# A fused attention + MoE kernel: second batch's softmax weights transposed by DMA, and the third expert unit's gathers ordered first

## The chip, the cores and the metric

One core of a Trainium2 chip runs the whole program. The metric is the device time of one execution in microseconds; several executions are timed and their median counts.

## The reference

Three layers follow each other on 1536 tokens (2 batches of 768) of width 512.

1. Attention with 8 heads of 64, scores `q k^T / 8` plus a bias that falls linearly with distance, kept only where the key is one of 8 global tokens or lies 0 to 95 places back; softmax; product with `v`.
2. A dense feed-forward layer: RMS norm, `silu(xn w_gate) * (xn w_val)`, times `w_out` (512 to 1536 and back).
3. A mixture of 8 experts (512 to 1024 and back, ReLU): a noisy router picks two experts per token, the token's two outputs are added with softmax weights of the two logits.

`top2 = argpartition(-noisy_logits, 2)[:, :2]` means that a small error upstream can send a token to another expert, which is why most matrix products run as three products of split halves (high x high, high x low, low x high).

## The kernel before, in words

**Attention.** Tokens come in 12 tiles `ti` of 128; tiles 0 to 5 are the first batch (`ti < F32T`), 6 to 11 the second. The eight heads of a tile are done in four pairs `pr`; a *unit* `u = 4*ti + pr` is one tile and one pair, 48 in all. A unit goes through three functions. `scores` (L409) multiplies on PE into a PSUM bank, adds the bias and finds the row minimum on DVE (L429, tile `s`), and takes the exponential on ACT (L432, tile `p`). `turn` (L437) transposes `p` on PE in blocks of 128x128 (L445): four blocks for a pair, or two where the tile is the first of its batch (one block of keys in place of two). In the second batch it then makes two half-precision tiles out of PSUM, a high part on ACT (L456) and the rest on DVE (L457). `values` (L465) multiplies these with `v` (L494, twenty products of 64 columns). When a tile's four pairs are done it is normalised (L502, then `rms`, L568) and `norm` (L586) transposes it for the next layer (tiles `xTh`, `xTl`, L595 and L596).

**Order.** `slot(n, part)` (L509) writes the order down: slot n holds `turn(n-1)`, `scores(n)` and `values(n-2)`, and at n % 4 == 2 the `norm` of the tile before. Slots 0 to 11 are written out by `early` (L536); the rest are dealt out by `side` (L1161) between the matmuls of the dense layer, eight for each of its first visits. `VISITS` (L132) lists the dense layer's visits: the first six take two token tiles each through the hidden chunks 0 to 3 (functions `up` L686, `hidden` L697, `down` L710). The framework then orders each engine's queue by a timeline of its own, so a slot can run well after the place where it is written; on the chip each queue is strictly in order. The sixth visit can't start before the last tile's `norm`.

**Loads.** SP's queue issues all plain loads and the transposing DMAs that exist already (L975 for gathered tokens `hg`, L1132 for expert outputs `ob`). The output is cleared by one 3 MB write from a zero tile (`clear_out`, L268), issued in the third visit.

**Experts.** `route` (L787) ranks the tokens of a group; for each assignment it scatters token number and weight into the table `metad` (L911, POOL). Nine `Unit`s of gathered tokens follow: units 0 and 1 are the same expert in two parts, units 2 to 8 one expert each. A unit's steps are `fetch` (L936: its part of the table, tile `me`, by SP), `slots` (L943: indices `ic` on POOL, L952), `gather` (L958: one indirect DMA from POOL per 128 tokens, from `x2d` for units up to 2, from the halved copy `x2p` for later ones), `turn` (L977: four PE transposes per 128 tokens, L990, then `gh` on ACT and `gl` on DVE, L993 and L994), and `run` (L1003) with eight steps f of `up` (L1022) and `down` (L1039, L1062). `halve` (L741) writes `x2p`: a copy on POOL into `hw` (two buffers) and a store by SP. `late` (L1233) routes the last group, halves the last four token tiles, and orders the first eight weight loads of unit 2 (`moe2_weights`, L919); then the loop at L1244 runs the units, with `side(f)` (L1248) ordering the next unit's fetch, slots, gathers, turns and weights. During unit 1 it does this for unit 2:

```
if i == 1:
    if f == 0:
        nxt.slots()
    if 1 <= f <= len(nxt.tiles):
        nxt.gather(f - 1)
```

Of the kernel before, what the change touches and what calls it, by code (L numbers as in the profile page):

```python
# [107 lines left out]
def fused(ctx: ExitStack, tc: tile.TileContext, q, k, v, n_global, n_local, w_gate, w_val, w_out,  # L108
# [55 lines left out]
    def build_bias():  # L164
        rel = sb.tile([P, 2 * P], F32, name="rel", tag="n2", bufs=N2)
        msk = sb.tile([P, 2 * P], F32, name="msk", tag="s", bufs=4)
        tmp = at.tile([P, 2 * P], F32, name="tmp", tag="p", bufs=4)
# [5 lines left out]
        rel0 = at.tile([P, P], F32, name="rel0", tag="p", bufs=4)  # L173
        msk0 = at.tile([P, P], F32, name="msk0", tag="p", bufs=4)
# [44 lines left out]
    blank = sb.tile([P, P], BF16, name="blank")  # L219
    nc.vector.memset(blank, 0.0)  # L220
# [47 lines left out]
    def clear_out():  # L268
        zero = at.tile([P, P], F32, name="zero", tag="p", bufs=4)
        nc.gpsimd.memset(zero, 0.0)  # L270
        nc.sync.dma_start(out.rearrange("(p t) (c d) -> p (t c) d", p=P, d=P),
                            zero.rearrange("p (o d) -> p o d", o=1).broadcast_to([P, NT // P * DC, P]))
# [136 lines left out]
    def scores(u, wide):  # L409
# [8 lines left out]
        pp = []  # L418
# [7 lines left out]
        for t in range(2):  # L426
# [4 lines left out]
            p = at.tile([P, 2 * P], F32, name=f"p{ti}_{h}", tag="p", bufs=4)  # L431
            state["e"] = nc.scalar.activation(p[:, :W], s[:, :W], AF.Exp, scale=-1.0, bias=mx[:, h:h + 1],  # L432
                                              accum_out=sm[:, h:h + 1]).ins
            pp.append(p)
        state["p", u] = pp

    def turn(u, wide):  # L437
# [5 lines left out]
        for t in range(2):  # L443
            for j in range(nblk):
                seq(nc.tensor.transpose(p4[:, t, j, :], pp[t][:, j * P:(j + 1) * P], ident))  # L445
        if ti < F32T:
            pf = at.tile([P, 2, 2, P], F32, name=f"pf{ti}_{pr}", tag="pt", bufs=2)
            if pr % 2 == 0:
                nc.scalar.activation(pf[:, :, :nblk], p4[:, :, :nblk], AF.Copy, scale=PSC)
            else:  # L450
                nc.vector.tensor_scalar(pf[:, :, :nblk], p4[:, :, :nblk], PSC, None, op0=ALU.mult)
            state["pt", u] = (pf[:, 0], pf[:, 1])
            return
        pair16 = at.tile([P, 2, 2, 2, P], F16, name=f"ph{ti}_{pr}", tag="pt", bufs=2)
        ph, pl = pair16[:, 0], pair16[:, 1]
        nc.scalar.activation(ph[:, :, :nblk], p4[:, :, :nblk], AF.Copy, scale=PSC)  # L456
        nc.vector.scalar_tensor_tensor(pl[:, :, :nblk], p4[:, :, :nblk], PSC, ph[:, :, :nblk],  # L457
                                       op0=ALU.mult, op1=ALU.subtract)
        state["pt", u] = (ph, pl)
# [49 lines left out]
    def slot(n, part):  # L509
# [16 lines left out]
        else:  # L526
# [4 lines left out]
            if ("pt", n - 2) in state:  # L531
# [835 lines left out]
```

## Time and profile before

| | us |
|---|---|
| median of 3 timed runs | 776.04 (775.14 to 782.92) |
| the profiled execution, device time | 777.18 |
| its span, first to last instruction | 775.5 |

The rows below come from that one execution. PE is the matmul engine, PEld its weight loads, DVE, ACT and POOL the vector, scalar and general engines, SP the engine that issues most DMAs. "busy" is the time in which at least one instruction of the engine is in flight; a matmul's duration overlaps with the next one's, so the time that one takes from PE is read from start to start. "idle before <-X" is the time the engine stood before an instruction and what released it. L numbers are lines of the kernel.

### The profile page before, as it was taken

The page shows a single profiled execution, that of the slowest core. Times are in us where ns is not written, and L with a number is a line of the kernel's source. Part 1 is how long each engine was busy: PE and PEld are TensorE (multiplying, and loading weights), DVE is VectorE, ACT ScalarE, POOL GpSimd, SP SyncE. Part 2 cuts the span into 40 slices and gives each one's busy share as a digit, 9 for nine tenths or more (in the row PEclk, how much of TensorE's full clock was granted, in tenths as well). Part 3 has the DMA queues.
Part 4 walks back from the last instruction along what each step waited for, and adds up shares of the span by engine and source line. Part 5 has one row for each costly group of instructions (what it writes and reads, how often), then busy time and mean ns, then how long its engine had stood idle before and what let it go on. Part 6 is the DMA issues. An engine that isn't in the chain of part 4 may idle for free. (4 is left out here: it accounts for less than half of the span.)

```text
span 775.5 us, 13632 instructions
## 1 busy us (share of the span) xinstructions
PE 747.3 (96%) x4851; PEld 675.6 (87%) x4851; DVE 480.6 (62%) x1104; ACT 407.1 (53%) x854; POOL 325.5 (42%) x357
## 2 busy tenths in 40 slices
PE   9899999999999999999999999799999999999993
PEld 5788989999798888889999988678999999999993
DVE  7988776766477889433535568544555656556642
ACT  6777566665444344113332455435575857676640
POOL 3367741332376557111542145352244545453511
PEclk9999999999999999999999999999999999999997
DMA  7554332250233330002243626896686989999211
GB/s 194 140 177 110 104 107 52 55 177 2 82 109 109 108 109 28 0 19 91 56 56 57 216 29 148 277 303 188 164 203 148 294 176 292 250 300 189 78 40 37
DMA packets 159864, 102.22 MB, mean 132 GB/s; under 512 B 90897, under 2 KB 142097, under 8 KB 159792
## 3 DMA queue, kind: packets, MB, share of 16 engines
q1 hardware_dynamic: 150944, 78.84, 40.2%
q0 software_dynamic: 7120, 19.32, 8.2%
q10 hardware_dynamic: 1728, 3.15, 1.5%
q8 instruction: 40, 0.66, 0.4%
q14 instruction: 32, 0.26, 0.1%
HBM read 75.23 MB, written 16.49 MB: 118 GB/s over the span
## 5 line engine op out<-in xcount | busy, mean ns | idle before, releaser
L1022 PE MATMUL pz<-gh,sa 128*128 128x256 f32 (+7 forms) x576 | 154.5, 337 | 1.5 <-ACT gh L993 0.8
L1022 PEld LDWEIGHTS pz<-gh,sa 128*128 128x128 f32 x576 | 104.1, 189 | 6.6 <-POOL sa L677 1.0
L1022 PE MATMUL pz<-gl,sa 128*128 128x256 f32 (+7 forms) x288 | 96.4, 336 | 0.8 <-DVE gl L994 0.8
L720 PE MATMUL acc<-wo,dh 128*128 128x512 f32 x288 | 89.0, 400 | 1.0 <-ACT dh L706 1.0
L1062 PE MATMUL ac<-zh,sb 128*128 128x480 f32 (+4 forms) x320 | 84.8, 357 | 0.0
L693 PE MATMUL pz<-xTh,wg 128*128 128x256 f32 x352 | 75.4, 289 | 2.3 <-ACT wg L644 1.3
L1029 ACT ACTIVATE zh<-pz 128x256 fp32r<-128x256 f32 (+7 forms) x72 | 35.1, 487 | 78.6 <-PE pz L1022 78.5
L1030 DVE SCALAR_TENSOR_TENSOR zl<-pz,zh 128x256 fp32r<-128x256 f32 (+7 forms) x72 | 39.7, 551 | 57.4 <-ACT zh L1029 57.1
L693 PE MATMUL pz<-xTh,wv 128*128 128x256 f32 x352 | 75.0, 288 | 0.0
L693 PEld LDWEIGHTS pz<-xTh,wg 128*128 128x128 f32 x352 | 59.0, 192 | 4.4 <-ACT wg L644 1.5
L1095 POOL DMA_INDIRECT out_dram<-y,me x30 | 32.5, 1083 | 72.0 <-DVE y L1091 57.8
L1062 PEld LDWEIGHTS ac<-zh,sb 128*128 128x128 f32 x320 | 59.5, 188 | 3.4 <-ACT sb L673 0.2
L677 DVE TENSOR_TENSOR sb<-wab,sb 128x512 fp32r<-128x512 f32 x67 | 47.6, 711 | 22.9 <-ACT sb L673 21.1
L707 POOL TENSOR_TENSOR dl<-u,dh 128x256 fp32r<-128x256 f32 (+1 forms) x38 | 38.6, 1015 | 53.8 <-ACT dh L706 30.1
L673 ACT ACTIVATE sa<-wab 128x512 fp32r<-128x512 f32 x72 | 44.9, 625 | 28.5 <-PE ac L1062 14.1
L720 PEld LDWEIGHTS acc<-wo,dh 128*128 128x128 f32 x288 | 51.3, 189 | 9.8 <-ACT dh L706 1.6
L693 PEld LDWEIGHTS pz<-xTh,wv 128*128 128x128 f32 x352 | 58.6, 191 | 0.4
L1022 PEld LDWEIGHTS pz<-gl,sa 128*128 128x128 f32 x288 | 54.4, 189 | 3.5 <-DVE gl L994 1.2
L432 ACT ACTIVATE p<-s,mx 128x256 f32<-128x256 f32 (+1 forms) x96 | 46.2, 483 | 21.2 <-DVE mx L429 21.1
L720 PE MATMUL acc<-wo,dl 128*128 128x512 f32 x144 | 53.0, 399 | 0.2 <-POOL dl L707 0.2
L677 DVE TENSOR_TENSOR sa<-wab,sa 128x512 fp32r<-128x512 f32 x54 | 40.1, 745 | 20.8 <-ACT sa L673 20.2
L1062 PE MATMUL ac<-zl,sb 128*128 128x480 f32 (+4 forms) x160 | 52.4, 358 | 0.0
(254 smaller groups left out, 1873.0 us busy)
## 6 DMA issues: line engine op xcount, KB each, us to landing
wab<-in_moe_w_dram SPq DMA_DIRECT2D x128, 256.0 KB, 5.4
rg<-in_moe_w_gate_dram SPq DMA_DIRECT2D x12, 512.0 KB, 4.6
rv<-in_moe_w_val_dram SPq DMA_DIRECT2D x12, 512.0 KB, 3.7
ro<-in_moe_w_out_dram SPq DMA_DIRECT2D x12, 512.0 KB, 3.5
vn<-in_v_dram SPq DMA_DIRECT2D x12, 256.0 KB, 4.6
out_dram<-zero SPq DMA_DIRECT2D x1, 3072.0 KB
x2d<-x ACTq DMA_DIRECT2D x12, 256.0 KB, 7.6
x2p<-hw SPq DMA_DIRECT2D x12, 256.0 KB, 4.5
```

The costliest lines, as they stand in the source:

```text
L432: state["e"] = nc.scalar.activation(p[:, :W], s[:, :W], AF.Exp, scale=-1.0, bias=mx[:, h:h + 1], accum_out=sm[:, h:h + 1]).ins
L673: cp = nc.scalar.activation(wp[:, 0], src, AF.Copy)
L677: (nc.gpsimd if pool else nc.vector).tensor_sub(wp[:, 1], src, wp[:, 0].bitcast(F32))
L693: mm = nc.tensor.matmul(pz, a[:, cs], x[:, tt:tt + nt, c, :], start=(n == 0), stop=(n == 3 * DC - 1))
L707: (nc.gpsimd if ci < len(CHUNKS) - 1 else nc.vector).tensor_sub(dl, u, dh.bitcast(F32))
L720: nc.tensor.matmul(acc[t], a[:, tt], w, start=(f == CHUNKS[ci][0] and n == 0), stop=(end and n == 2))
L1022: mm = nc.tensor.matmul(pz[:, :cap], a[:, cs], x[:, c, :cap], start=(k == 0), stop=(k == 3 * DC - 1))
L1029: self.act = nc.scalar.activation(dh[:, :cap], pz[:, :cap], AF.Relu).ins
L1030: nc.vector.scalar_tensor_tensor(dl[:, :cap], pz[:, :cap], 0.0, dh[:, :cap].bitcast(F32), op0=ALU.max, op1=ALU.subtract)
L1062: nc.tensor.matmul(acc[c][:, :cap], w[:, c * P:(c + 1) * P], a[:, :cap], start=(f == 0 and k == 0), stop=(f == FB2 - 1 and k == 2))
L1095: st = nc.gpsimd.indirect_dma_start(out=out, out_offset=bass.IndirectOffsetOnAxis(ap=self.me[:m, s, 0:1], axis=0), in_=y[:m], in_offset=No ...
```

## The change

Attention, second batch: after the exponential (now written over `s`), ACT makes the high half-precision part of each head from SBUF and DVE the rest, into one tile `pp` of [128, 2 parts, 2 heads, 256 columns] with two buffers; one transposing DMA on SP's queue turns this tile (eight blocks, or four for the first tile of the batch) into `both`, which `values` reads. `turn` is left for the first batch alone. `values` of the second batch moves one slot later (n-3 in place of n-2), its `norm` too, and there is one slot more. The first batch's two `p` tiles of a pair become one tile.

Third unit: in `late` its `fetch` is ordered ahead of its eight weight loads, and these are put behind the fetch in SP's queue; its `slots` and all four gathers are ordered at f = 0 of unit 1; the last four `halve` copies are put behind the last of these gathers on POOL, unit 3's `slots` behind the last copy, and unit 3's first two weight loads behind the last store of a halved tile.

Elsewhere: the 3 MB clearing write moves to the ninth visit, from a zero tile that is set once at the start and also serves as `blank`.

```diff
@@ -415,7 +413,11 @@
         mx, sm = state["mx", ti], state["sm", ti]
         nb = nbias if ti % NB else nbias0
         psc = bank("s", wide, f"ps{ti}_{pr}")
-        pp = []
+        first = ti < F32T
+        if first:
+            pp = at.tile([P, 2, 2 * P], F32, name=f"p{ti}_{pr}", tag="p", bufs=2)
+        else:
+            pp = at.tile([P, 2, 2, W], F16, name=f"h{ti}_{pr}", tag="p", bufs=2)
         for t in range(2):
             h = pair(ti, pr)[t]
             sl = slice((h % 2) * D, (h % 2 + 1) * D) if ti < HALF else slice(0, P)
@@ -428,11 +430,18 @@
             s = sb.tile([P, 2 * P], F32, name=f"s{ti}_{h}", tag="s", bufs=4)
             state["s"] = nc.vector.tensor_tensor_reduce(s[:, :W], nb[:, h, :], psc[:, t * W:(t + 1) * W], 1.0, BIG * 10,
                                                         op0=ALU.add, op1=ALU.min, accum_out=mx[:, h:h + 1]).ins
-            p = at.tile([P, 2 * P], F32, name=f"p{ti}_{h}", tag="p", bufs=4)
-            state["e"] = nc.scalar.activation(p[:, :W], s[:, :W], AF.Exp, scale=-1.0, bias=mx[:, h:h + 1],
+            p = pp[:, t, :W] if first else s[:, :W]
+            state["e"] = nc.scalar.activation(p, s[:, :W], AF.Exp, scale=-1.0, bias=mx[:, h:h + 1],
                                               accum_out=sm[:, h:h + 1]).ins
-            pp.append(p)
-        state["p", u] = pp
+            if not first:
+                nc.scalar.activation(pp[:, 0, t], p, AF.Copy, scale=PSC)
+                nc.vector.scalar_tensor_tensor(pp[:, 1, t], p, PSC, pp[:, 0, t], op0=ALU.mult, op1=ALU.subtract)
+        if first:
+            state["p", u] = pp
+            return
+        both = at.tile([P, 2, 2, nblk, P], F16, name=f"ph{ti}_{pr}", tag="pt", bufs=2)
+        nc.sync.dma_start_transpose(both.rearrange("p x t j q -> p (x t j) q"), pp.rearrange("p x t c -> p (x t c)"))
+        state["pt", u] = both[:, 0], both[:, 1]
 
     def turn(u, wide):
         ti, pr = divmod(u, NP)
@@ -442,21 +451,13 @@
         p4 = ptt.rearrange("p (t j q) -> p t j q", t=2, j=2)
         for t in range(2):
             for j in range(nblk):
-                seq(nc.tensor.transpose(p4[:, t, j, :], pp[t][:, j * P:(j + 1) * P], ident))
-        if ti < F32T:
-            pf = at.tile([P, 2, 2, P], F32, name=f"pf{ti}_{pr}", tag="pt", bufs=2)
-            if pr % 2 == 0:
-                nc.scalar.activation(pf[:, :, :nblk], p4[:, :, :nblk], AF.Copy, scale=PSC)
-            else:
-                nc.vector.tensor_scalar(pf[:, :, :nblk], p4[:, :, :nblk], PSC, None, op0=ALU.mult)
-            state["pt", u] = (pf[:, 0], pf[:, 1])
-            return
-        pair16 = at.tile([P, 2, 2, 2, P], F16, name=f"ph{ti}_{pr}", tag="pt", bufs=2)
-        ph, pl = pair16[:, 0], pair16[:, 1]
-        nc.scalar.activation(ph[:, :, :nblk], p4[:, :, :nblk], AF.Copy, scale=PSC)
-        nc.vector.scalar_tensor_tensor(pl[:, :, :nblk], p4[:, :, :nblk], PSC, ph[:, :, :nblk],
-                                       op0=ALU.mult, op1=ALU.subtract)
-        state["pt", u] = (ph, pl)
+                seq(nc.tensor.transpose(p4[:, t, j, :], pp[:, t, j * P:(j + 1) * P], ident))
+        pf = at.tile([P, 2, 2, P], F32, name=f"pf{ti}_{pr}", tag="pt", bufs=2)
+        if pr % 2 == 0:
+            nc.scalar.activation(pf[:, :, :nblk], p4[:, :, :nblk], AF.Copy, scale=PSC)
+        else:
+            nc.vector.tensor_scalar(pf[:, :, :nblk], p4[:, :, :nblk], PSC, None, op0=ALU.mult)
+        state["pt", u] = (pf[:, 0], pf[:, 1])
 
     def grows(ti):
         for a, b in zip(state["own", ti - 1], state.pop(("own", ti - 2))):
@@ -528,10 +529,13 @@
                 scores(n, wide)
             if n % NP == 1 and n // NP + 1 < NT // P:
                 prep(n // NP + 1, wide)
-            if ("pt", n - 2) in state:
+            if n - 2 < F32T * NP and ("pt", n - 2) in state:
                 values(n - 2, wide)
-        if part and n % NP == 2 and n >= NP:
-            norm(n // NP - 1, state.pop(("x", n // NP - 1)), wide)
+            if n - 3 >= F32T * NP and ("pt", n - 3) in state:
+                values(n - 3, wide)
+        ti = n // NP - 1
+        if part and n >= NP and n % NP == (2 if ti < F32T or not windowed else 3):
+            norm(ti, state.pop(("x", ti)), wide)
 
     def early(n):
 
@@ -680,6 +684,7 @@
     x2t = {}
     tail = []
     halves2 = {}
+    halved = []
     marks = []
     accs = {}
 
@@ -743,7 +748,8 @@
         cp = nc.gpsimd.tensor_copy(hw[:, 0].rearrange("p (t n) -> p t n", t=2), x2t[ti].bitcast(U16).rearrange("p (n t) -> p t n", t=2))
         if behind is not None:
             follow(cp.ins, behind)
-        nc.sync.dma_start(x2p[ti * P:(ti + 1) * P, :], hw[:, 0])
+        st = nc.sync.dma_start(x2p[ti * P:(ti + 1) * P, :], hw[:, 0])
+        halved.append((cp.ins, st.ins))
 
     def merge(x3, words, m, behind):
         cp = nc.scalar.activation(x3[:, :, :m].bitcast(U16).rearrange("p c (q t) -> p t c q", t=2),
@@ -916,12 +922,16 @@
                 for o in slots_done:
                     tc.declare_no_dep(st.ins, o, reason="every assignment has a slot of its own")
                 slots_done.append(st.ins)
-    def moe2_weights(u, e, f):
+    def moe2_weights(u, e, f, behind=None):
         w = slab(f"a{u}_{f}")
-        nc.sync.dma_start(w.rearrange("p (c f) -> p c f", c=DC),
+        ld = nc.sync.dma_start(w.rearrange("p (c f) -> p c f", c=DC),
                           w1[bass.ds(e, 1), :, f * P:(f + 1) * P].rearrange("o (c p) f -> p (o c) f", p=P))
+        if behind is not None:
+            follow(ld.ins, behind)
         w = slab(f"b{u}_{f}")
-        nc.sync.dma_start(w, w2[bass.ds(e, 1), f * P:(f + 1) * P, :].rearrange("o p d -> p (o d)"))
+        ld = nc.sync.dma_start(w, w2[bass.ds(e, 1), f * P:(f + 1) * P, :].rearrange("o p d -> p (o d)"))
+        if behind is not None:
+            follow(ld.ins, behind)
 
     class Unit:
         def __init__(self, n, wkey, e, s0, cap):
@@ -937,10 +947,10 @@
             n, ns = self.n, len(self.tiles)
             me = sb.tile([P, NS, 2], I32, name=f"me{n}", tag="me", bufs=4)
             src = metad.rearrange("(e s p) t -> e p s t", e=E, p=P)[bass.ds(self.e, 1), :, self.s0:self.s0 + ns]
-            nc.sync.dma_start(me[:, :ns], src.rearrange("o p s t -> (o p) s t"))
+            self.got = nc.sync.dma_start(me[:, :ns], src.rearrange("o p s t -> (o p) s t")).ins
             self.me = me
 
-        def slots(self, ids=None):
+        def slots(self, ids=None, behind=None):
             n, ns = self.n, len(self.tiles)
             if self.me is None:
                 self.fetch()
@@ -949,7 +959,9 @@
             if ids is not None:
                 nc.vector.tensor_scalar(ic[:, :ns], ids, float(self.rows - 1), None, op0=ALU.min)
             else:
-                nc.gpsimd.tensor_scalar(ic[:, :ns], me[:, :ns, 0], self.rows - 1, None, op0=ALU.min)
+                op = nc.gpsimd.tensor_scalar(ic[:, :ns], me[:, :ns, 0], self.rows - 1, None, op0=ALU.min)
+                if behind is not None:
+                    follow(op.ins, behind)
             self.ic = ic
             self.gh = sb.tile([P, DC, CAP], F32R, name=f"gh{n}", tag="xTh", bufs=3)
             self.gl = sb.tile([P, DC, CAP], F32R, name=f"gl{n}", tag="xTl", bufs=3)
@@ -1139,7 +1151,7 @@
 
     if not windowed:
         small_loads()
-    U = NT // P * NP + 3
+    U = NT // P * NP + 4
     n = 0
     if windowed:
         early(-1)
@@ -1197,7 +1209,7 @@
                 clear_meta()
             if vi == 1 and f == 2 and windowed:
                 small_loads()
-            if vi == 2 and f == 1:
+            if vi == 8 and f == 4:
                 clear_out()
             if nt == 2:
                 pz = ps.tile([P, 512], F32, name=f"pz{t0}_{f}", tag="gv"[count % 2])
@@ -1232,13 +1244,12 @@
 
     def late():
         route(NG - 1)
-        for ti in range(G0[LEAD + 1], NT // P):
-            halve(ti, units[1].last.ins)
         for i in range(E - 1):
             units.append(Unit(2 + i, 1 + i, None, 0, CAPS[i]))
         name(units[2])
+        units[2].fetch()
         for f2 in range(AHEAD):
-            moe2_weights(1, units[2].e, f2)
+            moe2_weights(1, units[2].e, f2, units[2].got)
     late()
 
     for i, u in enumerate(units):
@@ -1250,10 +1261,12 @@
                 if i == 1:
                     if f == 0:
                         nxt.slots()
-                    if 1 <= f <= len(nxt.tiles):
-                        nxt.gather(f - 1)
+                        for s in range(len(nxt.tiles)):
+                            nxt.gather(s)
+                        for ti in range(G0[LEAD + 1], NT // P):
+                            halve(ti, nxt.last.ins)
                 elif i and f == (3 if i == 2 else 0):
-                    nxt.slots()
+                    nxt.slots(behind=halved[-1][0] if i == 2 else None)
                     for s in range(len(nxt.tiles)):
                         nxt.gather(s)
                 if i and f == 6 and i + 2 < len(units):
@@ -1274,7 +1287,7 @@
                     if 8 - len(nxt.tiles) <= f:
                         nxt.turn(f - 8 + len(nxt.tiles), u.act)
             if nw is not None and (i > 1 or f >= AHEAD):
-                moe2_weights(nw.wkey, nw.e, f)
+                moe2_weights(nw.wkey, nw.e, f, halved[-1][1] if i == 2 and f == 0 else None)
         u.run(side)
     fast.close()
```

## Rows read from the trace of the kernel before

**Rows 1.** The page, part 1 (busy) and part 2 (PE's line of 40 slices).

```profile
PE 747.3 (96%) x4851; PEld 675.6 (87%) x4851; DVE 480.6 (62%) x1104; ACT 407.1 (53%) x854; POOL 325.5 (42%) x357
...
PE   9899999999999999999999999799999999999993
```

**Rows 2.** Busy time by stretch: us, then busy per engine, PEclk, DMA share, GB/s.

```profile
100.00:204.00 104.00, 104.00 (x1100) 97.70 (x1099) 69.14 (x195) 63.43 (x178) 30.91 (x46) 1.00 0.24 65
...
494.66:499.00 4.34, 0.00 (x1) 0.03 (x1) 0.75 (x2) 0.44 (x1) 3.43 (x4) 1.00 0.97 323
499.00:503.25 4.25, 4.25 (x21) 4.06 (x22) 1.89 (x4) 2.05 (x4) 1.45 (x3) 0.60 0.91 258
```

**Rows 3.** Timeline of PE around one turn of four blocks.

```profile
126.69 0.63 PE L445 MATMUL pp<-ident,p 128*128 128x128 f32 x4
127.08 0.36 PE L693 MATMUL pz<-xTl,wv 128*128 128x256 f32 x1
```

**Rows 4.** Instructions by tile pp (ns min/median/max), then groups by line and form.

```profile
L456 ACT ACTIVATE ph<-pp x24: 363/596/598, 90.9 to 198.3; 128x512 f16<-128x512 f32 x20, 128x256 f16<-128x256 f32 x4
L457 DVE SCALAR_TENSOR_TENSOR ph<-pp,ph x24: 409/691/693, 91.5 to 199.0; 128x512 f16<-128x512 f32 x20, 128x256 f16<-128x256 f32 x4
...
L703 DVE SCALAR_TENSOR_TENSOR u<-u,pz 128x256 f32<-128x256 f32 x16 | 6.7, 419 | 0.5
L706 ACT ACTIVATE dh<-u 128x256 fp32r<-128x256 f32 x16 | 6.6, 415 | 4.5 <-DVE u L703 4.5
```

**Rows 5.** Landing of transposing DMAs by tile (ob, then hg); SP's queue.

```profile
DMA to landing us min/median/max: 2.7/2.8/4.4
...
DMA to landing us min/median/max: 3.4/5.7/7.7
...
551.92 5.34 SPq L1132 DMA_TRANSPOSE ob<-oT  x4
```

**Rows 6.** Timeline: scores of units 32 and 47, then unit 47 to the next layer.

```profile
123.89 0.36 PE L425 MATMUL ps<-kT,q0e 128*128 128x256 f32 x1
...
191.71 0.37 PE L425 MATMUL ps<-kT,q0o 128*128 128x256 f32 x1
...
194.81 0.49 ACT L432 ACTIVATE p<-s,mx 128x256 f32<-128x256 f32 x1
...
198.34 0.60 ACT L456 ACTIVATE ph<-pp 128x512 f16<-128x512 f32 x1 [1.30 <-PE pp L445]
...
211.01 0.51 PE L693 MATMUL pz<-xTh,wg 128*128 128x256 f32 x2 [1.00 <-ACT xTh L595]
```

**Rows 7.** Timeline of POOL, 473 to 499 us.

```profile
473.71 0.97 POOL L911 DMA_INDIRECT metad<-meta,si  x1 [0.31 <-issue]
...
487.87 0.24 POOL L952 TENSOR_SCALAR ic<-me 128x4 int32<-128x4 int32 x1 [6.90 <-DMA me<-metad]
491.45 1.37 POOL L743 COPY hw<-x 128x1024 uint16<-128x1024 uint16 x1 [3.34 <-DMA x2p<-hw]
...
493.98 1.08 POOL L965 DMA_INDIRECT xg<-x2d,ic  x1 [0.50 <-POOL ic L952]
```

**Rows 8.** Timeline: the scatter a group earlier, its fetch, and unit 2's fetch.

```profile
450.33 0.97 POOL L911 DMA_INDIRECT metad<-meta,si  x1 [0.30 <-issue]
...
457.49 0.37 SPq L940 DMA_DIRECT2D me<-metad  x1
...
484.73 0.37 SPq L940 DMA_DIRECT2D me<-metad  x1
```

**Rows 9.** Timeline of PE at the start of unit 2.

```profile
499.00 0.63 PE L990 MATMUL pg<-ident,xg 128*128 128x128 f32 x4 [4.34 <-DMA xg<-x2d,ic]
...
507.14 0.70 PE L1022 MATMUL pz<-gh,sa 128*128 128x480 f32 x2 [0.77 <-ACT gh L993]
508.66 0.48 PE L1022 MATMUL pz<-gl,sa 128*128 128x480 f32 x1 [0.82 <-DVE gl L994]
```

**Rows 10.** Timeline of SP's queue: the clearing write.

```profile
154.74 0.67 SPq L271 DMA_DIRECT2D out_dram<-zero  x1
```

More of the change, by code (lines that the diff above doesn't have):

```diff
@@ L166, in build_bias @@
         msk = sb.tile([P, 2 * P], F32, name="msk", tag="s", bufs=4)
-        tmp = at.tile([P, 2 * P], F32, name="tmp", tag="p", bufs=4)
+        work = at.tile([P, 2, 2 * P], F32, name="work", tag="p", bufs=2)
+        tmp, rel0, msk0 = work[:, 0], work[:, 1, :P], work[:, 1, P:]
         nc.gpsimd.iota(rel, pattern=[[-1, 2 * P]], base=P, channel_multiplier=1,
@@ L172, in build_bias @@
         nc.vector.tensor_mul(msk, msk, tmp)
-        rel0 = at.tile([P, P], F32, name="rel0", tag="p", bufs=4)
-        msk0 = at.tile([P, P], F32, name="msk0", tag="p", bufs=4)
         nc.vector.tensor_scalar(rel0, rel[:, P:], -float(n_local), None, op0=ALU.add)
@@ L218, in small_loads @@
         nc.sync.dma_start(nz, noise.rearrange("(t p) e -> p t e", p=P))
-    blank = sb.tile([P, P], BF16, name="blank")
-    nc.vector.memset(blank, 0.0)
+    zero = sb.tile([P, P], F32, name="zero")
+    nc.vector.memset(zero, 0.0)
+    blank = zero.bitcast(BF16)[:, :P]
     state = {}
@@ L268, in clear_out @@
     def clear_out():
-        zero = at.tile([P, P], F32, name="zero", tag="p", bufs=4)
-        nc.gpsimd.memset(zero, 0.0)
         nc.sync.dma_start(out.rearrange("(p t) (c d) -> p (t c) d", p=P, d=P),
```

## Prediction

> **What bounds the kernel now.** I read the page first: PE is busy 96% of the span and every slice but two stands at 8 or 9 tenths or more, while DVE has 62% and ACT 53% [rows 1]. So I look for two things: PE work that goes away where PE is full, and the places where PE stands. The stretches give both. From 100 to 204 us, where the second batch's attention runs between matmuls of the dense layer, PE is busy for 104.00 of 104.00 us, DVE for 69.1 and ACT for 63.4 [rows 2]: any PE time removed there counts, as long as the other engines keep up. From 494.66 to 499.00 PE does nothing, and in the 4.25 us behind it the mean granted clock is 0.60 [rows 2], that is, mostly the 1.2 GHz level in place of 2.4. The reader is to see in that stretch that DMA is at 0.97 and POOL at 3.43 of 4.34: PE stands for a gather [rows 9], and the gather for POOL [rows 7].
>
> **Part 1, the transposes of the second batch.** Removed from PE: five tiles x four pairs x four blocks and one tile x four pairs x two, 88 blocks. A turn of four begins at 126.69 and the next matmul at 127.08 [rows 3]: 0.39 us from start to start. Twenty such turns and four of half the size (taken at 0.20) make 8.6 us. PE is full around them, so this is path, not cover.
>
> Removed from ACT and DVE: 0.596 and 0.691 us a unit, the two tiles made out of PSUM. Added: two operations of 256 columns on each; the nearest rows take 0.415 (ACT, SBUF to SBUF) and 0.419 (DVE, out of PSUM) [rows 4]. That is +0.23 us on ACT and +0.15 on DVE a unit, some 5.6 and 3.6 us over 24 units. The stretch would be about 95 us long, with DVE at 73 and ACT at 69 of it: three quarters. Hidden, while PE stays the fuller engine; without that cover it is at most 5.6 us.
>
> Added on SP: 24 transposing DMAs. The trace has DMAs of the same full size (128 rows of 1024 two-byte elements, SBUF to SBUF): `ob` lands 2.8 us after issue (2.7 to 4.4), `hg`, issued among gathers and weights, 5.7 (3.4 to 7.7); four in a row hold SP's queue for 5.34 us, 1.3 each [rows 5]. DMA is at 0.24 in the stretch [rows 2], so I take 2.8 and keep 7.7 as the upper end. Is there room? Units follow each other every 4.52 us (scores of unit 32 at 123.89, of unit 47 at 191.71, fifteen apart [rows 6]); without 0.39 us of PE each that is about 4.1. Two waits are new. The DMA of unit u needs a buffer of `both`, which `values(u-2)` frees, and must be back for `values(u)`, two slots or 8.2 us later; 2.8 us and a product fit. And ACT's copy of unit u needs a buffer of `pp`, which the DMA of u-2 frees. This one matters more, because ACT is in order: behind the copy stand the next exponentials and the dense layer's tanh, and behind those PE's `down`. By the written order the DMA of u-2 may start after `values(u-4)`, in slot u-1. From scores to the end of the exponentials is 3.6 us (191.71 to 194.81 + 0.49 [rows 6]); with the pitch of 4.1 and some 1.7 us for scores and products themselves (an estimate), ACT reaches the copy about 4.1 + 3.6 - 1.7 = 6.0 us after that start. At 2.8 us it doesn't wait. The transposes also share SP's queue with the loads of q, k and v, which wait there for buffers; by the planner's order such a load doesn't stand ahead of a transpose it depends on, and I cost it at nothing, with a slot's 4 us once per tile, 24 us, at the worst (the slower side).
>
> The end of this stage gives some of the gain back. PE waits 1.00 us at 211.01 for the last token tile's `xTh` [rows 6], 19.3 us after the scores of unit 47. So the attention's chain is already the later one there. If its pace is set by PE, it comes 8.6 us earlier with everything else and the wait stays; if it is set by DVE, ACT and the single bank of scores, PE only arrives earlier and waits longer, by up to the same 8.6 us. The unit's own chain hardly changes: before, from the end of the exponentials (195.3) over the turn to the end of ACT's copy is 3.6 us (198.34 + 0.60), and DVE's 0.69 follows; now two copies (0.83), DVE's last half (0.42) and the DMA (2.8) make 4.1 in place of 4.3. But `values` is written one slot later, and DVE and ACT are fuller. Between 0 and 8.6 I take 3.0, nearer to the low end, because PE was full for all of the 104 us. Part 1: 8.6 - 3.0 = 5.6 us.
>
> What speaks against such a move in the notes: the Trainium skill, page "VectorE: DVE Perf Modes", sections "The three transpose paths" and "Rules for kernel authors", gives 390 ns for a block of 128x128 on TensorE and 1309 ns by DMA, and advises TensorE where PSUM will do as the destination. By that price, as an estimate, eight blocks one after another take 10.5 us, past the 6.0 above, and the slower rival below would come to 776.0 + 4.5 x 24 - 15.3 = 868.7. This trace doesn't agree with such a sum: eight blocks land in 2.8 us [rows 5].
>
> **Part 2, the third unit.** Before: the last scatter of the table is issued at 473.71, unit 2's fetch goes out at 484.73 [rows 7, 8], behind it, while eight weight loads of 256 KB fill the rings. The numbers are there at 487.87, and POOL makes the indices at once; but the next thing in its queue is a `halve` copy that waits 3.34 us for a buffer and takes 1.37, then unit 3's indices, and the first gather leaves at 493.98 [rows 7]. It lands at 499.00 [rows 9]. Two causes, and the change takes up both. One group earlier a scatter issued at 450.33 let its fetch go at 457.49, 7.2 us later [rows 8]; so unit 2's fetch could go at about 480.9, its numbers land at 484.0 (3.1 us, as before), and with 0.24 us for the indices and 0.50 before the first gather [rows 7] that gather leaves near 485, the fourth, 1.4 us behind each other (1.08 and a pause of 0.3), near 489. With the 5.0 us of before the first lands at 490, the fourth by 494 to 497. PE was ready at 494.66. Even if the scatter is no faster, POOL's order alone brings the first gather to 488.6. So the wait of 4.34 us goes, and with it 4.25 x (1 - 0.60) = 1.7 us of halved clock. At the unit's first product PE waits 0.77 and 0.82 us more for `gh` and `gl` of the last rows [rows 9]; with the turns ahead of two `down` steps some of this goes too: I take 0.7 of 1.6. Sum 6.7 us, bounds 0 and 7.6. Late next is the landing of the eight weight loads, now issued behind the fetch, from 481 on: unit 2 needs the first converted near 500, which leaves over 15 us, and a gather of the same size lands in 5.0 with DMA at 0.97. Unit 3's weights start later as well, but a whole unit ahead of their use. The copies for unit 3 are later in POOL's queue than two of them are now, and one earlier than the last; unit 3's gathers, which need the stores, come well inside unit 2.
>
> **Edits at nothing.** The clearing write leaves 154.74 us [rows 10], where it would stand ahead of transposes on the same rings, for the ninth visit, where PE's slices are full [rows 1] and the next visits' weights are loaded ahead; it could cost its own length only if a weight load behind it were due at once. The paired `p` tile, the shared zero tile and the new slot at the end: a few tenths of a us either way.
>
> **Sum.** 777.18 - 5.6 - 6.7 = 764.9 for an execution like the profiled one, which stands 1.14 above the median of 776.04 (the span is 1.7 less than its time; what lies around it doesn't change). For the median: 763.7.
>
> **Rivals.**
> - *The attention chain sets the pace.* For it: PE already waits for it at 211.01, and units keep 4.5 us apart though scores, bias and exponential are only 3.6 long. Against it: PE never stands from 100 to 204. Then part 1 gives nothing and part 2 all: 776.0 - 6.7 = 769.3.
> - *The gathers still land late*, so the change doesn't do what it says: the weight loads now start just when the gathers do, and the fetch still waits for the scatter. For it: DMA at 0.97 in the stall. Against it: some 5 us between the first gather's landing as worked out and 494.66. Part 2 then gives about 1: 776.0 - 5.6 - 1.0 = 769.4.
> - *Slower: ACT stands before its copies.* If a transposing DMA takes longer than 6.0 us, ACT waits the rest in each unit, and PE behind it. At the 7.7 us of the slowest `hg` that is 1.7 x 24 = 41 us against 8.6 + 6.7 gained: 776.0 + 25.5 = 801.5. It decides from 6.0 + 15.3/24 = 6.6 us. Against it: DMA is at 0.24 there, and 2.8 is the value of an undisturbed transpose.
>
> **Chances.** The forecast 0.59 (its own range 757 to 768), the chain 0.16, the late gathers 0.14, slower 0.11. A measurement can tell about 1% from no change, that is below 768.3 or above 783.8. The first case counts as faster, the next two lie at the edge and count a little under half: faster 0.72, same 0.17, slower 0.11. The range goes from 757.0 (8.6 and 7.6 in full, the old end wait of 1.0, and some 1.8 that single turns can hide) to 774.0 (part 1 lost, part 2 at 2 us); above it lies the slower case, and little else.
>
> **What would show it.** Right: no transposes with tile `pp` on PE behind 90 us; transposing DMAs that land in about 3 us; PE still full in the attention stretch; a wait for `xTh` of some 2 to 5 us at the end of it; unit 2's first gather before 490 us (less what came before) and no PE wait for `xg`, with the clock at full. Wrong: PE waiting for `both` or for `dh` between 100 and 200 us, ACT idle ahead of its copies for DMA, landings over 6 us, or a wait for `xTh` near 9 us.

## The result and the profile after

| | before | changed |
|---|---|---|
| median, runs of one session | 777.51 us (4) | 770.62 us (4) |
| lowest to highest of the changed kernel | | 767.79 to 774.73 us |
| ratio, 95% interval | | 0.9895 (0.986 to 0.9929) |
| the profiled execution, its span | 777.18, 775.5 us | 774.73, 773.0 us |

The change takes 1.05% off, about 8.2 us, where 12.3 were forecast. A second session gave 771.98 us and 0.9906 (0.9872 to 0.994). The profiled execution is the longest of its four, so the comparisons below go by stretches and not by spans.

Busy time per engine and PE's line of slices, from the page of the changed kernel:

```profile
PE 738.5 (96%) x4763; PEld 668.9 (87%) x4763; DVE 492.3 (64%) x1128; ACT 408.5 (53%) x878; POOL 322.9 (42%) x356
...
PE   9889989999999999999999999996999999989993
```

Against [rows 1] PE has 88 instructions and 8.8 us of busy time less: the blocks of the second batch, near the price worked out for them. (Busy time also holds stretches at half clock; the eleven kernels without these 88 blocks have 734.3 to 741.4 us.) A new slice with a 6 stands near 530 us.

*Attention.* Stretches of the changed kernel, the columns as in [rows 2]; the last three belong to the third unit, below:

```profile
100.00:196.00 96.00, 94.49 (x1015) 89.08 (x1014) 76.47 (x226) 65.59 (x202) 32.48 (x45) 0.98 0.51 103
476.00:496.00 20.00, 19.70 (x128) 17.55 (x127) 15.09 (x23) 11.29 (x23) 8.74 (x9) 1.00 0.95 300
525.00:530.00 5.00, 5.00 (x24) 4.30 (x23) 2.55 (x4) 1.64 (x4) 0.22 (x1) 1.00 1.26 203
530.00:535.00 5.00, 2.85 (x13) 2.08 (x12) 0.00 (x0) 0.00 (x0) 0.00 (x0) 1.00 1.09 93
535.00:540.00 5.00, 1.00 (x3) 0.86 (x4) 1.02 (x2) 2.87 (x5) 1.91 (x2) 0.69 1.09 207
```

The tile `ph`, by its new transposing DMA, with who waited for it (us, times) and its landing:

```profile
L443 SPq DMA_TRANSPOSE ph<-h x24: 1191/1233/2095, 98.8 to 192.3; - x24
...
who waited for it (us, times):
  DVE x L503: 2.5, 1
  ACT h L437: 2.0, 4
  ACT wg L648: 1.9, 1
...
DMA to landing us min/median/max: 2.7/3.0/5.1
```

PE is still nearly full (94.49 of 96 us), the transposes land in 3.0 us and ACT's copies waited for them 2.0 us in all; the profile puts one more wait of ACT (1.9 us) and one of DVE (2.5 us) down to them. From the first dense product to the first one of the next hidden chunk it is 188.6 us in the profile before and 181.8 after; PE has no wait for `xTh` at the end of the stage any more, where [rows 6] had 1.00 us.

*The start*, where nothing was expected. SP's timeline of the changed kernel:

```profile
17.99 0.69 SPq L269 DMA_DIRECT2D out_dram<-zero  x1
19.09 9.36 SPq L309 DMA_DIRECT2D kn<-in_k_dram  x1
```

PE's timeline there:

```profile
32.49 0.63 PE L379 MATMUL pt<-ident,kn 128*128 128x128 f32 x4 [1.95 <-DMA kn<-in_k_dram]
...
40.23 0.66 PE L454 MATMUL pp<-ident,p 128*128 128x128 f32 x4 [1.93 <-ACT pf L457]
...
43.85 0.58 PE L698 MATMUL pz<-xTl,wg 128*128 128x256 f32 x1 [1.88 <-DVE xTl L600]
```

The 3 MB clearing write, ordered in the ninth visit by its place in the text, goes out at 18 us; before it was 154.74 [rows 10]. Behind it SP's queue stands 9.36 us at one load of `k` (0.37 before), PE waits three times for some 1.9 us, and from 41.9 us on, in the third of these waits, the clock is at the half level for 6.8 us: the products of that stretch are 0.21 us apart, against 0.12 at the full clock. The first dense product is at 41.6 us in place of 37.3.

*The third unit.* Its fetch on SP's timeline:

```profile
475.91 0.38 SPq L950 DMA_DIRECT2D me<-metad  x1
```

Its first gather on POOL's:

```profile
478.63 1.06 POOL L977 DMA_INDIRECT xg<-x2d,ic  x1 [0.47 <-POOL ic L962]
```

Its first product on PE's:

```profile
495.84 0.60 PE L1034 MATMUL pz<-gh,sa 128*128 128x480 f32 x2
```

No wait for `xg`, none for `gh` or `gl`, clock 1.00: from unit 1's first product to unit 2's it is 24.6 us in place of 31.6, near the 6.7 that were worked out. But from unit 2 to unit 3 it is 50.6 us in place of 43.1. ACT's timeline there:

```profile
537.13 1.34 ACT L755 ACTIVATE xc<-hg 128x1024 uint16<-128x1024 uint16 x1 [8.91 <-DMA hg<-xg]
538.34 0.60 ACT L677 ACTIVATE sb<-wab 128x512 fp32r<-128x512 f32 x1
```

PE's timeline behind it:

```profile
539.00 2.37 PE L1074 MATMUL ac<-zh,sb 128*128 128x480 f32 x5 [6.15 <-ACT sb L677]
```

ACT stands 8.91 us for the third transposed piece of unit 3's tokens. It was issued at 521.43 and ACT takes it up at 537.13, 15.7 us later; the landing of the fourth is on record, 13.9 us after its issue (7.7 was the longest in [rows 5]); the weight split `sb` is behind it in ACT's queue, and PE waits 6.15 us for that and runs at half clock behind it (five products of 480 columns in 2.37 us, against 1.24 in the step before). In the stretches above, 530 to 535 us has the DMA engines at 1.09 with 93 GB/s: busy, with little to show for it. In this execution unit 2's gain was given back.

### The profile page after: what moved, and what is told of

Same layout as the page of the kernel before. It is cut to its first block, busy times and chain, and to the rows that moved or that the text cites. A ratio compares the mean times of both kernels' runs of the same rounds, so it can differ in the third digit from the quotient of the medians.

```text
span 773.0 us, 13551 instructions
## 1 busy us (share of the span) xinstructions
PE 738.5 (96%) x4763; PEld 668.9 (87%) x4763; DVE 492.3 (64%) x1128; ACT 408.5 (53%) x878; POOL 322.9 (42%) x356
## 3 DMA queue, kind: packets, MB, share of 16 engines
q10 hardware_dynamic: 1728, 3.15, 1.3%
## 4 chain that ended last, share of the span: by engine, by line
PE 78%; DVE 5%; issue 5%; DMA 4%; ACT 3%; SPq 2%; POOL 1%; POOLq 0%; ACTq 0%; DVEq 0%
PE pz L698 16%; PE pz L1034 15%; PE acc L725 12%; PE ac L1074 10%; PE pg L698 5%; PE pv L698 5%; PE ac L1051 4%; PE ps L427 3%; DMA hg<-xg 2%; PE po L495 2%; PE lg L809 1%; PE pt L379 1%; SPq L932 1%; PE po L491 1%; ACT p L434 1%
## 5 line engine op out<-in xcount | busy, mean ns | idle before, releaser
L1074 PE MATMUL ac<-zh,sb 128*128 128x480 f32 (+4 forms) x320 | 86.5, 363 | 6.1 <-ACT sb L677 6.1
L1107 POOL DMA_INDIRECT out_dram<-y,me x30 | 33.8, 1128 | 64.5 <-DVE y L1103 57.8
L712 POOL TENSOR_TENSOR dl<-u,dh 128x256 fp32r<-128x256 f32 (+1 forms) x38 | 37.6, 990 | 44.5 <-ACT dh L711 24.6
L698 PE MATMUL pz<-xTl,wg 128*128 128x256 f32 x176 | 51.3, 291 | 1.9 <-DVE xTl L600 1.9
L725 PE MATMUL acc<-wo,dl 128*128 128x512 f32 x144 | 52.9, 396 | 0.0
L1051 PE MATMUL ac<-sb,zh 128*128 128x512 f32 (+1 forms) x176 | 50.9, 376 | 0.3 <-DVE sb L681 0.3
```

The lines of the kernel that those rows point to most:

```text
L698: mm = nc.tensor.matmul(pz, a[:, cs], x[:, tt:tt + nt, c, :], start=(n == 0), stop=(n == 3 * DC - 1))
L712: (nc.gpsimd if ci < len(CHUNKS) - 1 else nc.vector).tensor_sub(dl, u, dh.bitcast(F32))
L725: nc.tensor.matmul(acc[t], a[:, tt], w, start=(f == CHUNKS[ci][0] and n == 0), stop=(end and n == 2))
L1051: mm = nc.tensor.matmul(o, a[:, s * P:s * P + m], w[:, cuts(s)[x]], start=(f == 0 and k == 0), stop=(f == FB2 - 1 and k == 2)).ins
L1074: nc.tensor.matmul(acc[c][:, :cap], w[:, c * P:(c + 1) * P], a[:, :cap], start=(f == 0 and k == 0), stop=(f == FB2 - 1 and k == 2))
L1107: st = nc.gpsimd.indirect_dma_start(out=out, out_offset=bass.IndirectOffsetOnAxis(ap=self.me[:m, s, 0:1], axis=0), in_=y[:m], in_offset=No ...
```

## The experiments

Twelve runs, each timed beside the kernel before; a ratio is the run's median over that kernel's in the same session. "First product" is PE's first dense product, "u1" the first product of unit 1, and so on.

**1. The clearing write late.** On the changed kernel:

```diff
-        nc.sync.dma_start(out.rearrange(
+        st = nc.sync.dma_start(out.rearrange(
...
+        follow(st.ins, state["fed"])
```

(`state["fed"]` is the latest load of dense weights, set where these loads are issued.)

> The changed kernel with one edit: the 3 MB clearing write ordered in SP's queue behind the dense layer's latest weight load of the ninth visit, instead of at 18 us. Theory (the early write holds up the loads of q, k and v): the first dense matmul goes from 41.6 us back to about 37.3, the halved clock of 41.9 to 48.8 goes (3.4 us), so about 7 us less than the changed kernel, near 763.5. Rival (the reshaped p tile of the first batch, or chance in that one execution, makes the loss before 49 us): no difference, 770.6.

767.97 us, 0.9866 (0.9843 to 0.989). Between the two, and its interval overlaps that of the changed kernel. The write goes out at 242 us, and the waits for `kn` and `xTl` are gone. But this execution's PE ran its first matmuls at half their rate until 12.9 us, and its first `norm` came 3.7 us later. Numbers 10 and 12 below, one program, have it at 25.6 and 28.4 us, so this is chance of the execution; it hid most of the gain at the start in this profile (first product at 40.8 us, and at 36.9 to 37.1 in four others with the write late).

**2. The clearing write alone**, on the kernel before: the zero tile set once at the start, and the write ordered at `vi == 8 and f == 4`.

> The kernel before with the clearing edit alone (zero tile set once at the start, write at the ninth visit in program order), no other part of the change. Theory: the write has nothing to wait for and goes out about 18 us, the loads behind it come 9 us late, and the kernel is 5 to 8 us slower than before, near 784. Rival: as before, 777.5.

785.88 us, 1.0094 (1.0069 to 1.0119): 7.3 us slower, as expected. SP's timeline of this kernel has the same pair of rows:

```profile
18.70 1.06 SPq L270 DMA_DIRECT2D out_dram<-zero  x1
19.86 9.39 SPq L310 DMA_DIRECT2D kn<-in_k_dram  x1
```

Before, the zero tile shared the buffers of `p`, and POOL set it just ahead of the write. From the edit:

```diff
-        zero = at.tile([P, P], F32, name="zero", tag="p", bufs=4)
-        nc.gpsimd.memset(zero, 0.0)
```

From POOL's timeline of the kernel before:

```profile
154.50 0.21 POOL L270 MEMSET zero<- 128x128 f32 x1
```

So an edit that moves a write *later* in the text made it 136 us *earlier*. A later place in the text gives no reason for that; what is left is the tile: its setting held the write back, and without it nothing does.

**3 and 4. One part alone.** Part 1 with the late clearing write (the second part of the diff undone), and part 2 alone (on the kernel before).

> The changed kernel with the third unit's part undone and the clearing write late: the transposes of the second batch alone. Theory (PE sets the pace between 85 and 211 us): 6 to 9 us below before, near 770. Rival (the attention's chain sets the pace, and PE waits at its end): 0 to 2 below, 776. Second rival (DMA or the added work on ACT and DVE holds PE): at or above 777.5.

> The kernel before with the third unit's part alone. Theory: unit 2 starts 7 us earlier, and unit 2's wait for a transposed gather of unit 3 gives a part back: 3 to 7 us below before, near 772.5. Rival (the gain is given back in full, the waits of unit 2 being as long as those removed): 777.

Part 1: 770.92 us, 0.99 (0.9858 to 0.9941), 7.9 us, with an interval of 4.6 to 11.1. Part 2: 776.12 us, 0.9966 (0.9938 to 0.9994), 2.6 us of the 6.7. The profiled execution of the latter took 784.5 us and isn't used for lengths.

The profile of part 1 alone shows two things more. PE does wait for transposed tiles, 1.9 us in three waits between 100 and 200 us; two of the three in number 6 below, on PE's timeline:

```profile
107.61 0.20 PE L496 MATMUL po<-vn,ph 128*128 128x64 bf16 x1 [0.65 <-DMA ph<-h]
...
156.40 0.20 PE L496 MATMUL po<-vn,ph 128*128 128x64 bf16 x1 [1.62 <-DMA ph<-h]
```

All seven profiles with part 1 and the write late have such waits, 1.5 to 2.8 us in all; the four with the write early have at most 0.2. And though part 2 is left out, PE has no wait for `xg` here; it stands in unit 0 instead:

```profile
471.34 0.50 PE L1052 MATMUL ac<-sb,zh 128*128 128x512 f32 x1 [1.82 <-ACT zh L1042]
```

From unit 0's first product to unit 2's this profile has 57.8 us and that of number 2, with the same wait, 58.6; the one before, with the stall of 4.34 us, has 59.5. With part 2 ahead it is 52.6 to 53.0 in six profiles (the changed kernel, 5, 6, 8, 9 and 10) and 55.6 and 55.8 in two that have the wait in unit 0 (12 and 11). So the stall that part 2 removes isn't in every execution: up to unit 2 it gains 6.6 us without the wait in unit 0 (59.5 to 52.9) and some 2.5 with it (58.2 to 55.7). Runs 1 to 4, 11 and 12 were on one chip, the other six on two others; the wait of 1.8 to 2.0 us in unit 0 is in five profiles of the first (not in 1) and in none of the others. Why is open.

**5 to 8. Why unit 3 is late.** The changed kernel again, and three variants of experiment 1. Number 6:

```diff
-                moe2_weights(nw.wkey, nw.e, f, halved[-1][1] if i == 2 and f == 0 else None)
+                moe2_weights(nw.wkey, nw.e, f)
```

Number 7 is number 6 with unit 2's fetch back behind its weights. Number 8 is experiment 1 with unit 4's indices made on DVE, behind unit 3's last `gl`:

```diff
-            if ids is not None:
+            if n == 4:
+                op = nc.vector.tensor_scalar(ic[:, :ns], me[:, :ns, 0], self.rows - 1, None, op0=ALU.min)
+                follow(op.ins, units[3].low.ins)
+            elif ids is not None:
```

> The changed kernel as it stands, a second time, beside the variants below. Theory (the change itself makes unit 3 late, because unit 3's weights are held until 500 us and then come in one clump together with its gathers and transposes): PE again stands 4 to 7 us for the tokens hg at the end of unit 2, unit 2's start to unit 4's start is again 87 to 90 us (82.3 in the kernel before), and the median stays at 768 to 771 us. Rival (it was the chance of the one execution profiled): the wait is under 2 us, those two units take 82 to 84 us, and the time is near 765 us.

> The changed kernel with the clearing write behind the dense layer's latest load (as in the earlier variant that ran in 768 us), and with unit 3's first two weight loads no longer put behind the last store of a halved tile. Theory (the held weights come in a clump and push the transposes hg): unit 3's weights go out from about 490 us, the PE wait for hg at the end of unit 2 falls from 2.5 (6.2 in the first profile of the change) to under 1 us, unit 2's start to unit 4's start falls from 86 to 82 to 83 us, and the time to about 764 us. Rival (the DMA engines are full from 475 to 540 us whatever the order, so that unit 3's operands can't be there earlier; and the last store, now behind weights, makes the gathers late): the wait stays or grows, 767 to 770 us.

> As the variant before, and unit 2's fetch back behind its eight weight loads in SP's queue: of the second part of the change only POOL's order is left (gathers first, halved copies behind them, unit 3's indices behind the copies). Theory (the order on POOL is what counts): the first gather leaves near 487 instead of 479 us, unit 2 still starts without a wait for xg over 1 us, the next units are as in the kernel before (82 to 83 us for two), and the time is about 764 us, the same as with the fetch ahead. Rival (the fetch has to be ahead): PE waits 2 us or more for the tokens of unit 2 and runs at half clock behind it, and the time is 767 to 769 us.

> The variant with the late clearing write and the whole second part of the change, but unit 4's indices are made on DVE behind the last piece of unit 3's tokens, so that none of unit 4's gathers can run beside unit 3's transposes. Theory of the gathers (they share the DMA engines with the transposes, whose packets are small, and each slows the other): the transposes land within 8 us, the PE wait for hg falls from 2.5 to under 1 us, and the time to about 764.5 us. Rival (the transposes are late because weights were issued ahead of them): the wait stays at 2 us or more and the time at 767 to 769 us.

| | us | ratio | u1 to u2 | u2 to u4 | unit 0 to u4 |
|---|---|---|---|---|---|
| before | 779.0 | | 31.6 | 82.3 | 141.8 |
| 5, changed again | 771.98 | 0.9906 (0.9872 to 0.994) | 25.1 | 85.0 | 138.0 |
| 6, weights free | 763.95 | 0.9798 (0.9764 to 0.9832) | 25.0 | 82.4 | 135.3 |
| 7, POOL's order only | 765.8 | 0.9847 (0.9809 to 0.9885) | 30.5 | 81.2 | 139.7 |
| 8, gathers behind | 767.05 | 0.984 (0.9805 to 0.9875) | 25.0 | 82.8 | 135.7 |

(The lengths in the first line are from the one profile before; its time is the median beside runs 5 to 8.) Number 5: the transposes are late again (10.8 us at most) and POOL stands 7.5 us for one before a gather of unit 4, but this time PE hardly waits for ACT; it stands 2.4 us in unit 3 for a weight split of POOL (89.8 us from u2 to u4 in the first profile, 85.0 now). So the give-back is there again, by another wait, and its size varies. Number 7, on PE's timeline, shows what the fetch behind the weights does:

```profile
482.78 0.63 PE L1003 MATMUL pg<-ident,xg 128*128 128x128 f32 x4 [1.67 <-DMA xg<-x2d,ic]
486.43 1.08 PE L1003 MATMUL pg<-ident,xg 128*128 128x128 f32 x4 [3.03 <-DMA xg<-x2d,ic]
```

The eight weight loads are in front of the fetch there, so the gathers leave 12.3 us after unit 1's start (476.45 us), where number 6 has 8.3 and the changed kernel 7.4; the first lands 6.1 us after its issue, no later than in number 6 (6.7). From u1 to u2 this costs 5.5 us; the intervals of the two times overlap. Numbers 6 and 8 both have two nearly undisturbed units, as both theories asked. Number 6 is faster than the changed kernel beyond both intervals, and than experiment 1, from which it differs in the weights alone (0.9866), as well; these ran in different sessions.

**9. Unit 7.** A second loss, of 1.8 to 2.0 us of PE at unit 7, stood in number 6 and most of the other profiles with part 2. DVE's timeline in number 6:

```profile
684.16 3.53 DVE L998 TENSOR_TENSOR gl<-xc,gh 128x512 fp32r<-128x512 f32 x1 [1.68 <-ACT gh L997]
```

POOL's:

```profile
684.60 2.53 POOL L682 TENSOR_TENSOR sa<-wab,sa 128x512 fp32r<-128x512 f32 x2
```

And PE's, at the first products of unit 7:

```profile
687.74 0.61 PE L1035 MATMUL pz<-gl,sa 128*128 128x384 f32 x2 [1.80 <-DVE gl L998]
```

Number 9 is number 6 with unit 7's splits on DVE:

```diff
-        pool = u == 0 and f < 5 if key[0] == "b" else u > 2 and f < 3
+        pool = u == 0 and f < 5 if key[0] == "b" else u > 2 and f < (0 if u == 7 else 3)
```

> The variant with the late clearing write and unit 3's weights free (763.95 us), with the three weight splits that POOL makes for unit 7 made on DVE instead. In every profile with the second part of the change DVE's piece gl at the start of unit 7 (L998) takes 3.5 to 3.7 us in place of 0.68, with POOL at two weight splits in just that time, PE waits 1.8 to 1.95 us and mostly runs at half clock for 3.4 us behind it; in the kernel before POOL begins these two splits 0.8 us after that piece. Theory (DVE and POOL hold each other up when both work on SBUF operands, and the new order only shifted POOL's gathers of the output some 0.8 us forward): the piece takes 0.7 us, the wait at unit 7 falls to under 0.8 us, the start of unit 6 to the start of unit 7 falls from 34.0 to about 33.5 us and from there to the start of unit 8 from 35.4 to about 34 us, and the time by 2 to 3.5 us, to 761 to 762 us. Rival (the long piece is a wait for something else, such as the reading of gh): it stays at 3.5 us, no change in time.

763.64 us, 0.9799 (0.9754 to 0.9845). The piece takes 0.69 us and PE doesn't wait; from u7 to u8 it is 33.3 us in place of 35.4. The 2 us are seen in the profile and lie below what the medians of two sessions tell apart.

DVE's timeline in number 9, the same piece:

```profile
681.24 0.69 DVE L998 TENSOR_TENSOR gl<-xc,gh 128x512 fp32r<-128x512 f32 x1
```

**10 to 12. Is it the held weights?** Number 10 and, once more, 12: the changed kernel with only the edit of number 6, the clearing write still early. Number 11: the edits of 1, 6, 8 and 9 together.

> The changed kernel as it stands (the clearing write still at 18 us), only unit 3's first two weight loads no longer behind the last store of a halved tile. Theory (two separate terms: the clearing write early costs some 4.6 us before the first dense product at 41.7 in place of 37.1 us, the held weights cost 4 to 7 us at unit 3): first dense product still near 41.7, unit 2's start to unit 4's start 82 to 83 us, time about 767.5 us, between the changed kernel (771.98) and the variant with both mended (763.95). Rival (the held weights alone explain it and the start only shifts slack): about 764 us. Other rival (the clearing write is all of it): about 771 us.

> Four mends together on the changed kernel: clearing write behind the dense layer's latest load, unit 3's weights free, unit 4's indices on DVE behind unit 3's tokens, unit 7's three weight splits on DVE. Theory (the transposes of unit 3 are late because other transfers run beside them, and ACT, in order, holds PE behind them): no PE wait over 0.5 us between unit 2 and unit 4, those two units in 82 to 83 us, from unit 1's start to unit 4's start about 107.5 us (113.9 in the kernel before, 114.4 and 110.1 in the two profiles of the change), unit 7 without a wait over 0.8 us, time about 761 us. Rival (with unit 3's weights free, unit 4's gathers no longer matter): the same as the variant without the move of unit 4's indices, 763.6 us.

> The changed kernel with only unit 3's weights free, a second time: its first profile had PE standing 6.2 us in unit 2 behind ACT, which stood 9.0 us for the first transpose hg, while the same program for these units with the late clearing write had 0.9 and 3.7 us. Theory (a chance of the transfers in that execution: which of them come in the way of the transposes varies from run to run): this time ACT waits less than 6 us and PE less than 3, and unit 1's start to unit 4's start is 107 to 111 us in place of 115.5; time 767 to 771 us. Rival (the early clearing write changes something for these units in every execution): again 6 us and 115 us.

770.7 us, 0.9897 (0.985 to 0.9944), and 771.87 us, 0.9896 (0.986 to 0.9932): with the clearing write early, free weights gain nothing that can be measured. Number 11: 766.88 us, 0.9832 (0.9794 to 0.9871), no better than 6 and 9. ACT's timeline at the first transposed piece of unit 3, in number 10:

```profile
529.44 1.34 ACT L755 ACTIVATE xc<-hg 128x1024 uint16<-128x1024 uint16 x1 [8.95 <-DMA hg<-xg]
```

And in number 12, another execution of the same program:

```profile
524.37 1.37 ACT L755 ACTIVATE xc<-hg 128x1024 uint16<-128x1024 uint16 x1 [0.87 <-DMA hg<-xg]
```

A wait of 9.0 us in one and 0.9 in the other (the longest of PE's there: 6.2 and 0.6). So the held weights are not the cause by themselves, as I had it: the late transposes come and go from execution to execution. That it hangs on how the transfers meet is likely and not shown; which of the transfers beside them (weights, unit 4's gathers, the reading of old output) costs most stays open as well, since no run separates these with a firm sign. Also open is why free weights gain 5 us beside the late write (1 and 6) and nothing beside the early one.

## Why the prediction was right and where it failed

**The transposes on PE, 8.6 us: right.** PE has 88 matmuls fewer. From the first product to the next chunk's first, the profiles of the change and its variants with part 1 have 179.4 to 183.3 us, 181.2 on average over eleven; without it 188.6 and 191.6. Like with like, that is 7.9 us with the write not early (188.6 against 180.7 on average over seven) and 9.4 with the write early (191.6 against 182.1 over four).

**"Between 0 and 8.6 I take 3.0": failed.** This was the gain said to be given back as a longer wait for `xTh`; that wait is in none of the eleven profiles with part 1. The attention chain was not the later one: PE set its pace, and the stage is shorter by nearly all of what was taken off PE. (Experiment 2, without part 1, has no wait for `xTh` either, so its absence alone proves little; the lengths do.) Part 1's own timing, 7.9 us, points the same way, but its interval doesn't exclude 5.6. What was given back came in another place that the prediction had listed as a sign of being wrong: PE waits for the transposed tiles, 1.5 to 2.8 us, where the write is late. The rival in which the chain sets the pace (769.3) falls, and so does the slower one: 3.0 us a transpose, ACT's copies 2.0 us late in all, far from the 6.6 us a transpose from which it decides.

**"Edits at nothing ... for the ninth visit": failed.** I read the place in the text as the time. [rows 10] gave the time, 154.74, and the kernel's text the reason: the write stood behind a tile's buffer, and the change took that tile away. Cost: 7.3 us alone (experiment 2). Inside the change, the four timings with the write at 18 us average 0.9898 and the six with part 2 and the write late 0.9830, which is 5.3 us of 779; these six also differ in other edits. The closest pairs give 2.2 to 3.1 us (changed kernel and 1) and 7.7 (10 and 6).

**Part 2, "Sum 6.7": right to unit 2's start against the profile before, then failed.** The time from scatter to fetch was 6.6 us, the gather left at 478.63, the stall and its half clock were gone: 7.0 us. One thing that failed is that the sum took the stall of one profile for that of every execution: experiments 2 and 3 don't have it, and there the gain up to unit 2 would be some 2.5. The other is "unit 3's gathers, which need the stores, come well inside unit 2". They did, at 502.98; but their transposes were issued 43.6 us after unit 1's start, where they were at 42.8 before, while unit 2 had begun 7 us sooner. Unit 3's tokens didn't move with unit 2, and the slack that was there before no longer covered a transpose of 13.9 us. Of 6.7 us, 2.6 remain by experiment 4, and 2.6 by the difference of experiments 1 and 3 (0.9866 and 0.99, whose intervals overlap). How much of the missing 4.1 belongs to which of the two failures is open. The rival "gathers land late" gave nearly the right time for a different reason: unit 2's gathers were early.

**The sum again.** 7.9 for part 1, 2.6 for part 2, less some 2 to 7 for the clearing write: 3.5 to 8.5 us, against 8.2 and 7.3 measured. That the forecast came near is partly luck: one error made it too small (the 3.0) and two too large.

**The fastest version timed** is the change with the clearing write held to the end of the loads and unit 3's weights free: 763.95 us, 0.9798, with or without unit 7's splits on DVE (0.9799).

## What to carry to other kernels

Where a framework orders the queues itself, a transfer's place in the text is no place in time: ask what its data and buffers still wait for once the edit is made, and tie it to something if it must be late. When a stall goes, work out the time at which the next stage's operands arrive as an absolute time: here it didn't move with the stage before it. Read the stall in more than one profile of the kernel before you count on its whole length. Look along the in-order engine that consumes a transfer for what stands behind it: here PE waited for a weight split that was ready, behind a copy that wasn't.

## What the runs showed of the hardware

- DVE's piece `gl` of 512 columns takes 0.68 us alone and 3.53 to 3.67 when two weight splits of POOL (1.3 us each) begin 0.4 to 0.6 us after it; it ends only after they have. A piece of 32 columns takes 3.15 in the same way (number 9, at 645.25). In all fourteen profiles, every such piece over 1 us in the units overlaps a POOL split and every piece that overlaps one takes over 1 us. With the splits moved to DVE (experiment 9) it is 0.69.
- A transposing DMA of 256 KB landed in 3.0 us in the attention stretch with DMA at 0.51, and in up to 13.9 us beside gathers and weight loads at 1.26 and 1.09, where all transfers together moved 93 to 207 GB/s.
- The granted clock was at the 1.2 GHz level around some of PE's waits (in the changed kernel from 536.9 us for 6.8 us around the wait of 6.15, and from 41.9 us for 6.8 us around that of 1.88) and not around others (1.95 us at 694.60 in the same profile, 1.80 at 687.74 in number 6).
- At the start of an execution PE has a slow form that the granted clock doesn't show. From 5 to 12.5 us it makes 48 to 50 matmuls in ten of the fourteen profiles and 25 or 26 in four (numbers 1, 3, 8 and 12), all at a clock shown as 1.00; four scores of 64x128 take 0.71 us in number 10 and 1.22 in number 12, one program. With the write late the first dense product is then at 40.3 to 41.7 us in place of 36.9 to 37.1 (one profile of each kernel can't average this out); with it early, numbers 10 and 12 have it at 42.5 and 42.6, no difference.
